# Chunked attention followed by a gated MLP: q in 1 KB runs, V products directly behind exp, turns of x ahead of all loads in the SyncE queue

## The chip, the cores and the metric

The kernel runs on one core of one Trainium2 chip. The metric is the device time of one execution in microseconds (us). A profile shows one execution; its span is about 1.7 us shorter than the device time of the same run.

## The reference

64 independent attention sequences (8 batches, 8 heads, 576 tokens, head size 64) attend within chunks of 64 tokens. The heads are put side by side into x (4608 tokens, 512 wide), and a gated MLP follows:

```python
scores = scale * np.matmul(q_c, k_c.transpose(0, 1, 2, 4, 3))   # per chunk of 64
attn = softmax(scores); out = np.matmul(attn, v_c)
x = out.transpose(0, 2, 1, 3).reshape(B * S, H * D)             # 4608 x 512
h = x @ w_in                                                    # 512 -> 2048
g = h * (1.0 / (1.0 + np.exp(-beta * h)))
return g @ w_out                                                # 2048 -> 512
```

Inputs and output are float32 in HBM; the kernel computes in bf16.

## The kernel before

x is cut into nine blocks, 0 to 8, of 512 tokens (block 8 collects the last 64 tokens of every batch). For each block TensorE does the *projections* (`mm1`, 64 matmuls of 512 columns) and the *output products* (`mm2`, 64 more). The attention of block b is woven into the output products of block b-1. It has these steps:

- 64 small *score* matmuls, then four exp on ScalarE;
- two halves of *V products*, 32 small matmuls each;
- normalization on VectorE, which makes x in four parts of 128 tokens;
- four DMA transposes, the *turns of x*, issued by SyncE. The projections of block b read the turned x (`xT`).

A list of (time, function) pairs is sorted, and each engine's queue is filled in that order. One time unit is one group of four output products or projections. SyncE issues every load of q, k, v and every turn from one in-order queue, so a load that stands before a turn there holds it up.

```python
def attention(blk, T):                     # T = 32 * blk - 16
    for u in range(2): at(T + 0.6, scores, blk, u)
    for i in range(4): at(T + 1 + 0.1 * i, exp, blk, i)
    for j in range(2):
        for m in (2 * j, 2 * j + 1):
            for u in range(2):
                at(T + 4.6 + 4 * j, attend, blk, m, u, A, 2 * (m % 2) + u)   # V products
            at(T + 4.7 + 4 * j, normalize, blk, m, (0, 1), A, 2 * (m % 2))
            at(T + 4.8 + 4 * j, turn_x, blk, m)

def prepare(blk, T):                       # loads, casts, turns of q and k
    for m in range(4):
        # ... (blocks 2 and 3 have lists of their own)
        late = 17.5 if blk in (4, 5) else 0
        when = (T - 48 + m, T - 44 + m, T - 40 + m + late), ...   # loads of q, k, v
        ...

def load(blk, name, m):                    # 128 tokens x 8 heads: runs of 64 floats, 256 B
    # ...
    drams[name][b, :, t:t + n, :].rearrange("h t d -> t h d")
```

The softmax here doesn't subtract the row's maximum and nothing guards it: scores larger than these inputs give would overflow.

Of the kernel before, what the change touches and what calls it, by code (L numbers as in the profile page):

```python
# [158 lines left out]
def bass_chunk_attention__then__act_swish_beta_kernel(nc, q, k, v, w_in, w_out, beta, out):  # L159
# [7 lines left out]
    with ExitStack() as es:  # L167
# [6 lines left out]
        warm = sb("warm", [128, 1], F32)  # L174
        beta_raw = sb("beta_raw", [128, 8, 2], F32)
        beta_half = sb("beta_half", [128, 8, 2], F32)
# [9 lines left out]
        x_sb = sb("x_sb", [128, 4, 512], BF16)  # L186
        xT = sb("xT", [128, 2, NC, 512], BF16)
        NTT = 4
        tt = sb("tt", [128, NTT, 512], BF16)
        g2 = sb("g2", [128, NT, 512], BF16)  # L190
        NOS = 3
        ostage = sb("ostage", [128, NOS, 512], F32)

# [19 lines left out]
        def make_identity():  # L213
            P.op("pool", lambda e: e.memset(warm0[:, :], 0.0), writes=[K("warm0")])
            P.op("pool", lambda e: e.memset(identity[:, :], 1.0), writes=[K("identity")])
            P.op("pool", lambda e: e.affine_select(
                out=identity[:, :], in_=identity[:, :], compare_op=ALU.is_equal, fill=0.0,
                base=0, pattern=[[-1, 128]], channel_multiplier=1),
                reads=[K("identity")], writes=[K("identity")])
            P.op("pool", lambda e: e.memset(vaug[:, :, :, 64:65], 1.0), writes=[K("ones")])  # L220

        def load_beta():
            def f(e):
                with nc.allow_non_contiguous_dma(reason="beta is tiny"):
                    return e.dma_start(beta_raw[:, :, :],
                                       beta.rearrange("(e p i) -> p e i", p=128, i=2))
            P.dma("sp", f, writes=[K("beta_raw")])

        def halve_beta():
            P.op("pool", lambda e: e.tensor_single_scalar(  # L230
                beta_half[:, :, :], beta_raw[:, :, :], 0.5, ALU.mult),
                reads=[K("beta_raw")], writes=[K("beta_half")])

# [43 lines left out]

        def load(blk, name, m):
            for r, n, b, t in pieces(blk, m):
                def f(e, r=r, n=n, b=b, t=t):  # L280
                    return e.dma_start(
                        stages[name][r:r + n, blk % 2, 512 * m:512 * m + 512].rearrange("p (h d) -> p h d", d=64),
                        drams[name][b, :, t:t + n, :].rearrange("h t d -> t h d"))
                P.dma("sp", f, writes=[K(name + "stage", blk % 2, m, r, v=blk)])

# [3 lines left out]
        def cast_qk(blk, name, m, eng):  # L289
            dst = cast[name][:, :].rearrange("p (h m x) -> p h m x", h=4, m=4)[:, :, m, :]  # L290
            src = stages[name][:, blk % 2, 512 * m:512 * m + 512].rearrange("p (h x) -> p h x", h=4)
            copy(eng, dst, src, stage_keys(blk, name, m),
                 [K(name + "cast", m, v=blk)] +
                 keys(name + "cast", (1, 2, 3) if blk == 2 and m == 0 else (), v=0))

# [46 lines left out]
        def scores(blk, u):  # L342
            for hp in (2 * u, 2 * u + 1):
                for m in range(4):
                    for h2, c2 in ((0, 0), (1, 1), (0, 1), (1, 0)):
                        bank, col = 2 * u + h2, ((hp % 2) * 4 + m) * 64

                        def f(e, hp=hp, h2=h2, c2=c2, bank=bank, col=col, m=m):
                            r = slice(64 * h2, 64 * h2 + 64)
                            t = slice(128 * m + 64 * c2, 128 * m + 64 * c2 + 64)  # L350
                            return e.matmul(A[64 * c2:64 * c2 + 64, bank, col:col + 64],  # L351
                                            turned["k"][r, hp, t], turned["q"][r, hp, t])
                        P.op("pe", f, reads=[K("qT", hp, v=blk), K("kT", hp, v=blk)],
                             writes=[K("A", bank, v=("s", blk))])

        def exp(blk, bank):
            P.op("act", lambda e: e.activation(E[:, bank, :], A[:, bank, :], AF.Exp, scale=0.125),  # L357
                 reads=[K("A", bank, v=("s", blk))], writes=[K("E", bank, v=blk)])
# [26 lines left out]
        def turn_x(blk, m):  # L385
            P.dma("sp", lambda e: e.dma_start_transpose(  # L386
                xT[:, blk % 2, :, 128 * m:128 * m + 128], x_sb[:, m, :]),
                reads=[K("x", m, u, v=blk) for u in range(2)],
                writes=[K("xT", blk % 2, m, v=blk)])

        def turn_x_pe(blk, m, ps, bank, eng):
            key = pkey(ps, bank)
            mid = ps[:, bank, 0:256].bitcast(BF16).rearrange("p (h t) -> p h t", h=4)
            for hp in range(4):
                P.op("pe", lambda e, hp=hp: e.transpose(  # L395
                    mid[:, hp, :], x_sb[:, m, 128 * hp:128 * hp + 128], identity[:, :]),
                    reads=[K("x", m, hp // 2, v=blk), K("identity")], writes=[K(*key, v=("x", blk, m))])
            copy(eng, xT[:, blk % 2, :, 128 * m:128 * m + 128], mid,
                 [K(*key, v=("x", blk, m))], [K("xT", blk % 2, m, v=blk)])

        def mm1(blk, t, lo=0, hi=512):
            bank, T = t % 4, NT * blk + t
            e0, i = t // 2, t % 2
            for c in range(NC):
                P.op("pe", lambda e, c=c: e.matmul(  # L405
                    F[:, bank, lo:hi], w_in_bf[:, c, 256 * e0 + i:256 * e0 + 256:2],
                    xT[:, blk % 2, c, lo:hi], start=(c == 0), stop=(c == NC - 1)),
                    reads=[K("w_in", e0, c)] +
                    [K("xT", blk % 2, m, v=blk) for m in range(lo // 128, hi // 128)],
                    writes=[K("F", bank, v=("h", T))])  # L410
# [30 lines left out]
        def attention(blk, T):  # L441
# [4 lines left out]
            for j in range(2):  # L446
                for m in (2 * j, 2 * j + 1):
                    for u in range(2):
                        at(T + 4.6 + 4 * j, attend, blk, m, u, A, 2 * (m % 2) + u)
                    at(T + 4.7 + 4 * j, normalize, blk, m, (0, 1), A, 2 * (m % 2))  # L450
                    at(T + 4.8 + 4 * j, turn_x, blk, m)

        def prepare(blk, T):
            for m in range(4):
                if blk == 2:
                    when = (26 + m, 30 + m, (34, 34.5, 35.5, 36)[m]), (30 + 0.8 * m, 34 + 0.4 * m, 40 + m), (33.5, 35.7)
                elif blk == 3:
                    when = (36.1 + 0.1 * m, (37.5, 37.6, 53, 53)[m], 58.1 + 0.1 * m), (44 + m, 48 + m + 6 * (m // 2), 70 + m), (58, 60)
                else:
                    late = 17.5 if blk in (4, 5) else 0  # L460
                    when = (T - 48 + m, T - 44 + m, T - 40 + m + late), \
                        (T - 41 + m, T - 37 + m, T - 17 + m + late / 5), (T - 20, T - 18)
                for i, name in enumerate("qkv"):
                    at(when[0][i], load, blk, name, m)
                    if name == "v":
                        at(when[1][i], cast_v, blk, m, "pool")
                    else:
                        at(when[1][i], cast_qk, blk, name, m, "pool")
                        if m == 3:
                            at(when[2][i], turn_qk, blk, name)  # L470

# [32 lines left out]
        at(-75, cast_w_in, 0, 1, ("pool", "pool"))  # L504
        at(-75, halve_beta)
        at(-75, cast_w_in, 1, 1, ("pool",))
# [97 lines left out]
```

## Time and profile before

| | before |
|---|---|
| device time, first three runs | 302.73 us median (302.0 to 303.44) |
| span of the profiled run | 300.8 us |
| first projection of block 0 / block 1 | 19.63 / 54.35 us |
| projections' start to projections' start, clean block | 29.90 us |
| the same into blocks 2, 5, 7 | 32.27, 31.23, 31.42 us |

The windows view of the kernel before follows, one line for each stretch from one block's first projection to the next one's (blocks 1-2, 2-3, 3-4, 4-5, 5-6, 6-7). The columns are the stretch, its length, then busy time (and instructions) of PE, PEld, DVE, ACT and POOL, then the granted TensorE clock, the DMA share and GB/s.

```profile
54.35:86.62 32.27, 30.34 (x272) 15.45 (x273) 14.57 (x25) 16.31 (x26) 9.97 (x17) 1.00 1.12 220
86.62:116.69 30.07, 30.05 (x256) 14.04 (x257) 14.41 (x24) 14.85 (x23) 7.25 (x12) 1.00 0.95 188
116.69:146.59 29.90, 29.90 (x257) 14.08 (x257) 14.41 (x24) 15.44 (x24) 7.36 (x12) 1.00 0.98 194
146.59:177.82 31.23, 30.06 (x257) 14.04 (x256) 14.41 (x24) 16.04 (x25) 9.81 (x16) 1.00 1.10 218
177.82:207.72 29.90, 29.89 (x256) 14.12 (x257) 14.41 (x24) 14.85 (x23) 7.30 (x12) 1.00 1.05 198
207.72:239.14 31.42, 30.06 (x258) 14.05 (x257) 14.41 (x24) 16.04 (x25) 7.36 (x12) 1.00 1.23 188
```

TensorE fills a clean block (29.90 of 29.90 us), so it is the limit there. VectorE and ScalarE are busy half the time. DMA is full (share about 1 and above). The surplus sits in three stretches, and the list of waits gives its cause (columns: us in total, times, longest):

```profile
PE F L405 <- DMA xT<-x_sb: 4.3, 3, 1.7
```

Three times TensorE was ready for the next block's projections and x had not been turned. The timeline of the kernel before around one of the three, at block 5, shows why. Its columns are start and length in us, the engine (SPq is SyncE's queue, DVE is VectorE), the line, the operation, out<-in (A and F lie in PSUM), shapes and count; in brackets stands how long the engine had been idle, and for what. DMA_DIRECT2D is a load, DMA_TRANSPOSE a turn.

```profile
163.90 5.03 SPq L281 DMA_DIRECT2D vstage<-in_v_dram  x4
165.61 0.70 PE L367 MATMUL A<-vaug,E 64*64 64x65 bf16 x32
166.34 0.69 DVE L379 TENSOR_TENSOR x_sb<-A,rden 128x512 bf16<-128x512 f32 x1
168.97 7.17 SPq L386 DMA_TRANSPOSE xT<-x_sb  x4
169.80 0.70 PE L367 MATMUL A<-vaug,E 64*64 64x65 bf16 x32
171.37 0.69 DVE L379 TENSOR_TENSOR x_sb<-A,rden 128x512 bf16<-128x512 f32 x1
177.82 2.53 PE L405 MATMUL F<-xT,w_in_bf 128*128 128x512 bf16 x11 [1.18 <-DMA xT<-x_sb]
```

Read it as a race. The first part of x is ready at 167.03 (166.34 + 0.69), but SyncE is still issuing v loads and comes to the turns at 168.97, 1.9 us late. The last part of x is ready at 172.06; TensorE wants all of it at 176.64 (177.82 - 1.18). Between these lie 4.6 us, in which the last turns must be issued and must land. They do not make it.

### The profile page before, as it was taken

How to read it: one execution, taken by the hardware profiler on the slowest of the kernel's cores; microseconds unless marked ns; L12 is line 12 of the kernel's file. 1: busy time of each engine (PE TensorE's matmuls, PEld its weight loads, DVE VectorE, ACT ScalarE, POOL GpSimd, SP SyncE). 2: the span in 40 equal slices, each digit the busy share in tenths (PEclk: the TensorE clock that was granted, in tenths of full speed). 3: DMA queues.
4: the chain of work that ended last, by engine and by line, in shares of the span. 5: the costliest groups of instructions: out<-in, count | busy, mean ns of one | idle time of the engine just before them, and what ended most of it. 6: DMA issues, size and time to landing. Idle time of an engine off the chain costs nothing.

```text
span 300.8 us, 5817 instructions
## 1 busy us (share of the span) xinstructions
PE 283.0 (94%) x2432; PEld 138.7 (46%) x2432; DVE 140.4 (47%) x238; ACT 148.6 (49%) x230; POOL 74.6 (25%) x118
## 2 busy tenths in 40 slices
PE   2789999999979999999999989999999899999994
PEld 1555454645434444444444534454444344444441
DVE  1547835483318442844274408541754076218600
ACT  3538624785138714871477037713871277228511
POOL 1347646332211521142114411440142100000000
PEclk9999999999999999999999999999999999999999
DMA  7999999999999948996999999998999950230033
GB/s 230 258 352 403 360 314 228 254 220 203 242 204 224 216 123 203 213 214 143 203 232 207 238 168 225 217 184 166 200 170 185 200 95 2 70 110 31 2 70 70
DMA packets 154489, 57.53 MB, mean 191 GB/s; under 512 B 142176, under 2 KB 147296, under 8 KB 154464
## 3 DMA queue, kind: packets, MB, share of 16 engines
q1 hardware_dynamic: 149216, 47.73, 79.0%
q10 hardware_dynamic: 5248, 9.44, 10.6%
q8 instruction: 19, 0.31, 0.5%
q14 instruction: 6, 0.05, 0.1%
HBM read 36.71 MB, written 9.44 MB: 153 GB/s over the span
## 4 chain that ended last, share of the span: by engine, by line
PE 85%; DMA 6%; DVE 4%; ACT 2%; SPq 1%; issue 1%
PE F L405 41%; PE F L424 36%; DMA xT<-x_sb 5%; PE A L367 3%; PE A L351 2%; DVE x_sb L379 2%; DMA kstage<-in_k_dram 2%; SPq L386 1%; ACT E L357 1%; DVE rden L377 1%; PE A L329 1%; PE F L329 1%; DVE g L417 0%; ACT tt L414 0%; PE F L395 0%
## 5 line engine op out<-in xcount | busy, mean ns | idle before, releaser
L417 DVE SCALAR_TENSOR_TENSOR g<-tt,F 128x512 bf16<-128x512 bf16 x144 | 98.5, 687 | 77.8 <-ACT tt L414 77.7
L405 PE MATMUL F<-xT,w_in_bf 128*128 128x512 bf16 (+1 forms) x608 | 127.2, 370 | 4.7 <-DMA xT<-x_sb 4.3
L424 PE MATMUL F<-w_out_bf,g 128*128 128x512 bf16 x576 | 130.6, 379 | 0.0
L414 ACT ACTIVATE tt<-F,beta_half 128x512 bf16<-128x512 f32 x144 | 98.3, 687 | 32.7 <-PE F L405 32.4
L405 PEld LDWEIGHTS F<-xT,w_in_bf 128*128 128x128 bf16 x608 | 59.5, 99 | 71.2 <-ACT ostage L429 3.5
L424 PEld LDWEIGHTS F<-w_out_bf,g 128*128 128x128 bf16 x576 | 54.2, 98 | 62.4
L429 ACT ACTIVATE ostage<-F 128x512 f32<-128x512 f32 x36 | 21.5, 597 | 92.2 <-PE F L424 92.0
L260 POOL CAST vaug<-vstage 128x512 bf16<-128x512 f32 x36 | 22.8, 634 | 67.8 <-DMA vstage<-in_v_dram 57.6
L260 POOL CAST qcast<-qstage 128x512 bf16<-128x512 f32 x28 | 17.2, 613 | 52.7 <-DMA qstage<-in_q_dram 51.7
L377 DVE RECIPROCAL rden<-A 128x8 f32<-128x8 f32 (+1 forms) x36 | 7.2, 200 | 49.2 <-PE A L367 49.2
L260 POOL CAST kcast<-kstage 128x512 bf16<-128x512 f32 (+1 forms) x30 | 19.3, 642 | 30.6 <-DMA kstage<-in_k_dram 30.6
L379 DVE TENSOR_TENSOR x_sb<-A,rden 128x512 bf16<-128x512 f32 (+1 forms) x36 | 23.8, 662 | 1.2
L357 ACT ACTIVATE E<-A 128x512 bf16<-128x512 f32 x36 | 18.8, 601 | 8.4 <-PE A L351 8.4
L367 PEld LDWEIGHTS A<-vaug,E 64*64 64x64 bf16 x544 | 10.6, 109 | 8.3 <-issue 3.8
L367 PE MATMUL A<-vaug,E 64*64 64x65 bf16 x544 | 13.1, 195 | 0.8 <-ACT E L357 0.5
L260 POOL CAST w_in_bf<-wstage 128x1024 bf16<-128x1024 f32 (+1 forms) x9 | 8.3, 945 | 5.1 <-DMA wstage<-in_moe_w_in_dram 5.1
L351 PEld LDWEIGHTS A<-qT,kT 64*64 64x64 bf16 x576 | 6.4, 111 | 5.7 <-issue 3.4
L351 PE MATMUL A<-qT,kT 64*64 64x64 bf16 x576 | 7.9, 200 | 1.2 <-DVE kT L260 0.7
L329 PE MATMUL F<-identity,qcast 128*128 128x128 bf16 x16 | 2.0, 308 | 5.5 <-DVE qcast L260 5.5
L260 POOL CAST w_out_bf<-wstage 128x1024 bf16<-128x1024 f32 x6 | 6.1, 1041 | 2.9 <-DMA wstage<-in_moe_w_out_dram 2.0
L258 ACT ACTIVATE qT<-F 128x1024 bf16<-128x1024 bf16 x2 | 2.0, 1023 | 5.8 <-PE F L329 5.8
L260 DVE CAST qcast<-qstage 128x1024 bf16<-128x1024 f32 x4 | 2.7, 694 | 4.7 <-DMA qstage<-in_q_dram 4.7
(38 smaller groups left out, 38.7 us busy)
## 6 DMA issues: line engine op xcount, KB each, us to landing
vstage<-in_v_dram SPq DMA_DIRECT2D x32, 256.0 KB, 5.1
out_dram<-ostage ACTq DMA_DIRECT2D x32, 256.0 KB, 3.6
qstage<-in_q_dram SPq DMA_DIRECT2D x24, 256.0 KB, 5.0
kstage<-in_k_dram SPq DMA_DIRECT2D x24, 256.0 KB, 5.8
wstage<-in_moe_w_out_dram SPq DMA_DIRECT2D x4, 1024.0 KB, 11.9
wstage<-in_moe_w_in_dram SPq DMA_DIRECT2D x3, 1024.0 KB, 9.6
qstage<-in_q_dram SPq DMA_DIRECT2D x4, 512.0 KB, 9.7
kstage<-in_k_dram SPq DMA_DIRECT2D x4, 512.0 KB, 8.4
```

What stands on the lines that cost most here:

```text
L260: P.op(eng, lambda e: e.tensor_copy(dst, src), reads=r, writes=wr)
L329: P.op("pe", lambda e, h=h, i=i, c=c, mid=mid: e.transpose(mid[:, 512 * h + 128 * i:512 * h + 128 * i + 128], cast[name][:, c:c + 128], id ...
L351: return e.matmul(A[64 * c2:64 * c2 + 64, bank, col:col + 64], turned["k"][r, hp, t], turned["q"][r, hp, t])
L357: P.op("act", lambda e: e.activation(E[:, bank, :], A[:, bank, :], AF.Exp, scale=0.125), reads=[K("A", bank, v=("s", blk))], writes=[K("E" ...
L367: return e.matmul(ps[r, bank, 128 * (h % 4):128 * (h % 4) + 65], E[r, 2 * u + h % 2, col:col + 64], vaug[r, m, h, 0:65])
L377: P.op("dve", lambda e: e.reciprocal(rd, o[:, :, :, 64]), reads=r, writes=[K("rden", m, u, v=blk) for u in us])
L379: P.op("dve", lambda e: e.tensor_tensor(x_sb[:, m, 256 * us[0]:256 * (us[0] + n)].rearrange("p (b h d) -> p b h d", h=4, b=n), o[:, :, :, ...
L405: P.op("pe", lambda e, c=c: e.matmul(F[:, bank, lo:hi], w_in_bf[:, c, 256 * e0 + i:256 * e0 + 256:2], xT[:, blk % 2, c, lo:hi], start=(c = ...
L414: P.op("act", lambda e: e.activation(tt[:, T % NTT, :], F[:, bank, :], AF.Tanh, scale=beta_half[:, e0, i:i + 1]), reads=[K("F", bank, v=(" ...
L417: P.op("dve", lambda e: e.scalar_tensor_tensor(g2[:, t, :], tt[:, T % NTT, :], 1.0, F[:, bank, :], ALU.add, ALU.mult), reads=[K("F", bank, ...
L424: P.op("pe", lambda e, t=t: e.matmul(F[:, s, :], g2[:, t, 128 * s:128 * s + 128], w_out_bf[:, t, :], start=(t == 0), stop=(t == NT - 1)), ...
L429: P.op("act", lambda e: e.activation(ostage[:, N % NOS, :], F[:, s, :], AF.Copy, scale=0.5), reads=[K("F", s, v=("o", N))], writes=[K("o", ...
```

## The change

The intent is to have the turns land in time by three means, and to relieve the DMA. The diff, cut to its core:

```diff
 def attention(blk, T):
-    at(T + 4.6 + 4 * j, attend, ...)      at(T + 4.7 + 4 * j, normalize, ...)    at(T + 4.8 + 4 * j, turn_x, ...)
+    at(T + 4.1 + 2.5 * j, attend, ...)    at(T + 4.2 + 2.5 * j, normalize, ...)  at(T + 4.3 + 2.5 * j, turn_x, ...)
 def prepare(blk, T):                       # other lists of times
+    late = {3: 12}.get(blk, 0)
+    lq, lk = [T - 48 + late + u for u in range(2)], [T - 46 + late + m for m in range(4)]
+    lv = [T - 42 + late * 1.6 + m for m in range(4)]
+    ...
+    if spread(blk):                        # 2 <= blk < 8
+        at(lq[u], load_qk4, blk, "q", u)   # four tokens x 64 floats in one run: 1 KB
+        at(cq[u], cast_qk4, blk, "q", u, "pool")
 def scores(blk, u):                        # moving operand: four runs of 16 tokens
+    qq = turned["q"][r, 2*u:2*u+2, :].rearrange("d a (b h p) -> d h (a b) p", b=2, h=2)[:, hp % 2, :, 16*c:16*c+16]
 def exp(blk, bank):                        # puts the tokens in order while it reads PSUM
+    dst = dst.rearrange("k (g p i) -> k g p i", p=16, i=4)
+    src = src.rearrange("k (g i p) -> k g p i", p=16, i=4)
-xT = sb("xT", [128, 2, NC, 512], BF16)     # and five output stages instead of three
+xT = sb("xT", [128, NC, 512], BF16)
-beta_raw: one load of 128x8x2 (runs of 8 B)
+beta_raw: four loads of 8x64 (runs of 256 B) and two 32x32-block transposes on VectorE
```

On TensorE only 8 instead of 16 output products stand between the two halves of the V products; in SyncE's queue the four turns of x stand together, and from block 4 on a period carries four turns, the turns of the next q and k, then the loads of q, k, v of the block after.

More of the change, by code (lines that the diff above doesn't have):

```diff
@@ L174, in bass_chunk_attention__then__act_swish_beta_kernel @@
         warm = sb("warm", [128, 1], F32)
-        beta_raw = sb("beta_raw", [128, 8, 2], F32)
+        beta_raw = sb("beta_raw", [128, 64], F32)
+        beta_turned = sb("beta_turned", [128, 2, 32], F32)
         beta_half = sb("beta_half", [128, 8, 2], F32)
@@ L190, in bass_chunk_attention__then__act_swish_beta_kernel @@
         g2 = sb("g2", [128, NT, 512], BF16)
-        NOS = 3
+        NOS = 5
         ostage = sb("ostage", [128, NOS, 512], F32)
@@ L219, in make_identity @@
                 reads=[K("identity")], writes=[K("identity")])
+            P.op("pool", lambda e: e.memset(beta_raw[:, :], 0.0), writes=[K("beta_pad")])
             P.op("pool", lambda e: e.memset(vaug[:, :, :, 64:65], 1.0), writes=[K("ones")])
         def load_beta():
-            def f(e):
-                with nc.allow_non_contiguous_dma(reason="beta is tiny"):
-                    return e.dma_start(beta_raw[:, :, :],
-                                       beta.rearrange("(e p i) -> p e i", p=128, i=2))
-            P.dma("sp", f, writes=[K("beta_raw")])
+            for g in range(4):
+                P.dma("sp", lambda e, g=g: e.dma_start(
+                    beta_raw[32 * g:32 * g + 8, :],
+                    beta.rearrange("(e x) -> e x", e=8)[:, 64 * g:64 * g + 64]),
+                    reads=[K("beta_pad")], writes=[K("beta_raw", g)])
         def halve_beta():
+            for i in range(2):
+                P.op("dve", lambda e, i=i: e.transpose(beta_turned[:, i, :], beta_raw[:, i::2]),
+                     reads=[K("beta_raw", g) for g in range(4)], writes=[K("beta_turned", i)])
             P.op("pool", lambda e: e.tensor_single_scalar(
-                beta_half[:, :, :], beta_raw[:, :, :], 0.5, ALU.mult),
-                reads=[K("beta_raw")], writes=[K("beta_half")])
+                beta_half[:, :, :], beta_turned[:, :, 0:8].rearrange("p i e -> p e i"), 0.5, ALU.mult),
+                reads=[K("beta_turned", i) for i in range(2)], writes=[K("beta_half")])
         def load_w_in(e0, n):
@@ L275, in cast_w_out, with load @@
                      [K("w_out", t + x) for x in range(n)])
-        def load(blk, name, m):
+        def load(blk, name, m, eng="sp"):
             for r, n, b, t in pieces(blk, m):
@@ L283, in f @@
                         drams[name][b, :, t:t + n, :].rearrange("h t d -> t h d"))
-                P.dma("sp", f, writes=[K(name + "stage", blk % 2, m, r, v=blk)])
+                P.dma(eng, f, writes=[K(name + "stage", blk % 2, m, r, v=blk)])
         def stage_keys(blk, name, m):
@@ L293, in cast_qk, with spread @@
                  [K(name + "cast", m, v=blk)] +
-                 keys(name + "cast", (1, 2, 3) if blk == 2 and m == 0 else (), v=0))
+                 keys(name + "cast", (1, 2, 3) if m == 0 and blk in (2, B) else (), v=0))
+        def spread(blk):
+            return 2 <= blk < B
         def turn_qk(blk, name):
@@ L349, in f @@
                             r = slice(64 * h2, 64 * h2 + 64)
-                            t = slice(128 * m + 64 * c2, 128 * m + 64 * c2 + 64)
+                            c = 2 * m + c2
+                            t = slice(64 * c, 64 * c + 64)
+                            qq = turned["q"][r, hp, t]
+                            if spread(blk):
+                                qq = turned["q"][r, 2 * u:2 * u + 2, :].rearrange(
+                                    "d a (b h p) -> d h (a b) p", b=2, h=2)[
+                                    :, hp % 2, :, 16 * c:16 * c + 16]
                             return e.matmul(A[64 * c2:64 * c2 + 64, bank, col:col + 64],
-                                            turned["k"][r, hp, t], turned["q"][r, hp, t])
+                                            turned["k"][r, hp, t], qq)
                         P.op("pe", f, reads=[K("qT", hp, v=blk), K("kT", hp, v=blk)],
@@ L356, in exp @@
         def exp(blk, bank):
-            P.op("act", lambda e: e.activation(E[:, bank, :], A[:, bank, :], AF.Exp, scale=0.125),
+            dst, src = E[:, bank, :], A[:, bank, :]
+            if spread(blk):
+                dst = dst.rearrange("k (g p i) -> k g p i", p=16, i=4)
+                src = src.rearrange("k (g i p) -> k g p i", p=16, i=4)
+            P.op("act", lambda e: e.activation(dst, src, AF.Exp, scale=0.125),
                  reads=[K("A", bank, v=("s", blk))], writes=[K("E", bank, v=blk)])
@@ L386, in turn_x @@
             P.dma("sp", lambda e: e.dma_start_transpose(
-                xT[:, blk % 2, :, 128 * m:128 * m + 128], x_sb[:, m, :]),
+                xT[:, :, 128 * m:128 * m + 128], x_sb[:, m, :]),
                 reads=[K("x", m, u, v=blk) for u in range(2)],
-                writes=[K("xT", blk % 2, m, v=blk)])
+                writes=[K("xT", m, v=blk)])
         def turn_x_pe(blk, m, ps, bank, eng):
@@ L397, in turn_x_pe @@
                     reads=[K("x", m, hp // 2, v=blk), K("identity")], writes=[K(*key, v=("x", blk, m))])
-            copy(eng, xT[:, blk % 2, :, 128 * m:128 * m + 128], mid,
-                 [K(*key, v=("x", blk, m))], [K("xT", blk % 2, m, v=blk)])
+            copy(eng, xT[:, :, 128 * m:128 * m + 128], mid,
+                 [K(*key, v=("x", blk, m))], [K("xT", m, v=blk)])
         def mm1(blk, t, lo=0, hi=512):
@@ L406, in mm1 @@
                     F[:, bank, lo:hi], w_in_bf[:, c, 256 * e0 + i:256 * e0 + 256:2],
-                    xT[:, blk % 2, c, lo:hi], start=(c == 0), stop=(c == NC - 1)),
+                    xT[:, c, lo:hi], start=(c == 0), stop=(c == NC - 1)),
                     reads=[K("w_in", e0, c)] +
-                    [K("xT", blk % 2, m, v=blk) for m in range(lo // 128, hi // 128)],
+                    [K("xT", m, v=blk) for m in range(lo // 128, hi // 128)],
                     writes=[K("F", bank, v=("h", T))])
@@ L448, in attention @@
                     for u in range(2):
-                        at(T + 4.6 + 4 * j, attend, blk, m, u, A, 2 * (m % 2) + u)
-                    at(T + 4.7 + 4 * j, normalize, blk, m, (0, 1), A, 2 * (m % 2))
-                    at(T + 4.8 + 4 * j, turn_x, blk, m)
+                        at(T + 4.1 + 2.5 * j, attend, blk, m, u, A, 2 * (m % 2) + u)
+                    at(T + 4.2 + 2.5 * j, normalize, blk, m, (0, 1), A, 2 * (m % 2))
+                    at(T + 4.3 + 2.5 * j, turn_x, blk, m)
         def prepare(blk, T):
-            for m in range(4):
-                if blk == 2:
-                    when = (26 + m, 30 + m, (34, 34.5, 35.5, 36)[m]), (30 + 0.8 * m, 34 + 0.4 * m, 40 + m), (33.5, 35.7)
-                elif blk == 3:
-                    when = (36.1 + 0.1 * m, (37.5, 37.6, 53, 53)[m], 58.1 + 0.1 * m), (44 + m, 48 + m + 6 * (m // 2), 70 + m), (58, 60)
-                else:
-                    late = 17.5 if blk in (4, 5) else 0
-                    when = (T - 48 + m, T - 44 + m, T - 40 + m + late), \
-                        (T - 41 + m, T - 37 + m, T - 17 + m + late / 5), (T - 20, T - 18)
-                for i, name in enumerate("qkv"):
-                    at(when[0][i], load, blk, name, m)
-                    if name == "v":
-                        at(when[1][i], cast_v, blk, m, "pool")
-                    else:
-                        at(when[1][i], cast_qk, blk, name, m, "pool")
-                        if m == 3:
-                            at(when[2][i], turn_qk, blk, name)
@@ new lines, in prepare @@
+            if blk == 2:
+                lq, lk, lv = (26, 27), (30, 31, 32, 33), (34, 34.5, 35.5, 36)
+                cq, ck, cv = (28, 30), (34, 34.4, 34.8, 35.2), (40, 41, 42, 43)
+                turns = (33.5, 35.7)
+            else:
+                late = {3: 12}.get(blk, 0)
+                lq, lk = [T - 48 + late + u for u in range(2)], [T - 46 + late + m for m in range(4)]
+                lv = [T - 42 + late * 1.6 + m for m in range(4)]
+                cq, ck = [T - 41 + late + u for u in range(2)], [T - 39 + late + m for m in range(4)]
+                cv = [T - 13 + m for m in range(4)]
+                turns = T - 20, T - 18
@@ new lines, in prepare @@
+            for u in range(2):
+                if spread(blk):
+                    at(lq[u], load_qk4, blk, "q", u)
+                    at(cq[u], cast_qk4, blk, "q", u, "pool")
+                else:
+                    for m in (2 * u, 2 * u + 1):
+                        at(lq[u], load, blk, "q", m)
+                        at(cq[u], cast_qk, blk, "q", m, "pool")
+            for m in range(4):
+                at(lk[m], load, blk, "k", m)
+                at(ck[m], cast_qk, blk, "k", m, "pool")
+                at(lv[m], load, blk, "v", m)
+                at(cv[m], cast_v, blk, m, "pool")
@@ L473, in bass_chunk_attention__then__act_swish_beta_kernel @@
+            at(turns[0], turn_qk, blk, "q")
+            at(turns[1], turn_qk, blk, "k")
         first = (("q", 0), ("k", 0), ("q", 1), ("k", 1))
@@ L504, in bass_chunk_attention__then__act_swish_beta_kernel @@
         at(-75, cast_w_in, 0, 1, ("pool", "pool"))
-        at(-75, halve_beta)
+        at(-69.2, halve_beta)
         at(-75, cast_w_in, 1, 1, ("pool",))
```

## The prediction

> **What bounds the kernel now.** TensorE. The windows view gives PE 30.05 us busy of 30.07 us from projection start to projection start of a steady block (86.6 to 116.7 us), clock 1.00. The same period takes 31.07 us into block 5 (146.8 to 177.8), 31.26 us into block 7 (207.9 to 239.1) and 32.27 us into block 2. The list of waits names the surplus: PE's first projection waited for the transposed x, 4.3 us in 3 waits (timeline: 1.74, 1.18, 1.36 us at 86.6, 177.8, 239.1). PE's other idle time is the start (about 9 of the first 19.6 us) and the end (about 4 us), which the change hardly touches.
>
> **Why those waits.** The chain there: x by VectorE, two x turns issued by SyncE (1.22, 1.26 us), then 3.05, 4.50 and (block 2) 6.70 us of DMA. DMA is full: share 0.95 to 1.23 in these windows. In block 2 two k loads stand between the turns; into blocks 5 and 7 SyncE reaches the first turn about 2 and 1.3 us after x was ready, because eight v loads stood before it.
>
> **What changes.**
> 1. q of blocks 2 to 7 in 1 KB runs. In the trace a 256 B packet takes 23.0 ns on average, a 1 KB one 51.4. 1 MB of q costs 4096 x 23.0 / 16 = 5.9 us of DMA before, 1024 x 51.4 / 16 = 3.3 after: 2.6 us less per block, none directly on PE's path. The Trainium skill, "DMA: Bandwidth & Descriptors", Specifications, puts line rate at 512 B and more; the packets agree (11 against 20 GB/s per engine).
> 2. Its price: scores stream q in runs of 16 tokens, exp reads PSUM with a stride. I expect both unchanged (64 score matmuls in 0.69 us, exp 601 ns); no strided PSUM read by exp is in the trace. Slack: exps end at 72.2 us, V products start at 73.85.
> 3. Second half of the V products 8 instead of 16 matmuls after the first: 1.7 us earlier. Normalization frees its banks about 0.5 us before.
> 4. Four x turns together. Counted from the V products' start: x ready after 1.4 to 4.6 us, last turn issued by 6.5, landed by 9.5 to 11; PE needs it at 10.8. It just fits.
> 5. beta as four small loads plus two VectorE transposes: 1024 packets x 9.2 ns / 16 = 0.6 us of DMA saved, perhaps 1 us more SyncE issue. The start's chain does not contain it: near 0.
> 6. One xT buffer: the turn follows the last projection of the block before anyway. Free.
>
> **On the critical path:** only the 4.3 us of x waits. I expect 4.1 gone: 302.7 - 4.1 = 298.6 us. Range 297.2 to 300.4. Chances: faster by over 2% 0.05, within 2% 0.92, slower 0.03.
>
> **Signs.** Right: PE waits for transposed x below 0.5 us in all; every period from block 2 on 30.0 to 30.1 us; first projection still at about 19.6 us; DMA share per period down by about 0.08; score group 0.69 us, exp about 600 ns. Wrong: scores or exp slower; x turns landing over 4.5 us after the last issue; a PE wait for exp or normalization between the V products; first projections waiting for w_in.
>
> **What would break it.** A strided moving operand that halves the score rate costs 0.7 us x 6 = 4 us and eats the gain. A DMA backlog ahead of the x turns of block 2 or 3 (v of two blocks there) leaves a wait of 1 to 2 us.

## The result, and the profile after

The change runs in 298.8 us (median of 4 runs, 298.38 to 299.22), the kernel before in 302.37 us (4 runs). The ratio is 0.988, with a 95% interval of 0.9844 to 0.9917. Ratios here are the mean time of one kernel's runs over that of the other's of the same rounds, so they are not quite the ratio of the medians. The whole interval lies below 1, so the change is faster, but by less than 2%.

The windows view of the changed kernel, same stretches and columns as above:

```profile
55.27:85.57 30.30, 29.56 (x267) 15.60 (x273) 14.56 (x25) 15.46 (x25) 8.21 (x12) 1.00 1.03 210
85.57:116.19 30.62, 29.75 (x253) 14.03 (x256) 14.40 (x24) 15.97 (x25) 9.44 (x14) 1.00 1.14 224
116.19:146.09 29.90, 29.58 (x253) 14.12 (x258) 14.40 (x24) 14.92 (x24) 6.88 (x10) 1.00 0.97 196
146.09:175.99 29.90, 29.58 (x254) 14.09 (x257) 14.41 (x24) 15.45 (x24) 6.88 (x10) 1.00 0.89 193
175.99:205.88 29.89, 29.57 (x253) 14.08 (x256) 14.40 (x24) 15.45 (x24) 6.88 (x10) 1.00 0.97 195
205.88:235.78 29.90, 29.58 (x254) 14.11 (x256) 14.40 (x24) 15.45 (x24) 7.36 (x12) 1.00 1.16 192
```

The stretches into blocks 5 and 7 are clean now, and the one into block 2 lost 1.97 us. (PE's busy time reads 0.3 us less than the stretch because some matmul records are missing: 253 instead of 256.) The one into block 3 became 0.55 us longer. The list of waits of the changed kernel names what is left:

```profile
PE F L424 <- DMA xT<-x_sb: 0.6, 1, 0.6
```

The timeline of the changed kernel at block 5, to be read as the one above:

```profile
165.11 0.70 PE L386 MATMUL A<-vaug,E 64*64 64x65 bf16 x32
165.84 0.69 DVE L398 TENSOR_TENSOR x_sb<-A,rden 128x512 bf16<-128x512 f32 x1
166.56 6.27 SPq L405 DMA_TRANSPOSE xT<-x_sb  x4
167.57 0.70 PE L386 MATMUL A<-vaug,E 64*64 64x65 bf16 x32
169.14 0.69 DVE L398 TENSOR_TENSOR x_sb<-A,rden 128x512 bf16<-128x512 f32 x1
175.99 4.26 PE L424 MATMUL F<-xT,w_in_bf 128*128 128x512 bf16 x19
```

SyncE waits for x (it issues at 166.56, x was ready at 166.53). The last part of x is ready at 169.83, 6.2 us before TensorE wants it. It was 4.6 before, 1.6 us less. The second V products moved by 1.7 us; 0.15 us of it is not seen because TensorE lost that much more before than the list of waits shows (31.23 - 29.90 - 1.18).

**The account.** From block 1's first projection to the end, the kernel before takes 300.8 - 54.35 = 246.45 us and the changed one 297.5 - 55.27 = 242.23 us: 4.22 us less. The 0.92 us that separate this from the 3.3 us between the two spans were lost before block 1, in the start (54.35 against 55.27); that is put down to chance, the moment at which TensorE's full clock came (see the experiments on the start).

**The price of the 1 KB runs** was to be in scores and exp. The groups of both kernels (columns: count, busy us, mean ns of one, then idle time before) show none. Before:

```profile
L357 ACT ACTIVATE E<-A 128x512 bf16<-128x512 f32 x36 | 18.8, 601 | 8.4 <-PE A L351 8.4
L351 PE MATMUL A<-qT,kT 64*64 64x64 bf16 x576 | 7.9, 200 | 1.2 <-DVE kT L260 0.7
```

After:

```profile
L376 ACT ACTIVATE E<-A 128x512 bf16<-128x512 f32 x36 | 18.8, 601 | 8.4 <-PE A L366 8.4
L366 PE MATMUL A<-qT,kT 64*64 64x64 bf16 x576 | 7.9, 200 | 1.1 <-DVE kT L266 0.7
```

24 of the 36 exps (blocks 2 to 7) have the new form, and the four of each block take 592 to 619 ns in both kernels. Neither ScalarE's strided read of PSUM nor q in runs of 32 B, as TensorE now streams it, cost anything here.

### The profile page after: what moved, and what is told of

It reads as the page before. It is cut to its first block, busy times and chain, and to the rows that moved or that the text cites. A ratio compares the mean times of both kernels' runs of the same rounds, so it can differ in the third digit from the quotient of the medians.

```text
span 297.5 us, 5766 instructions
## 1 busy us (share of the span) xinstructions
PE 280.0 (94%) x2395; PEld 139.3 (47%) x2432; DVE 140.6 (47%) x240; ACT 148.5 (50%) x230; POOL 72.2 (24%) x107
## 4 chain that ended last, share of the span: by engine, by line
PE 81%; SPq 8%; DMA 6%; issue 2%; DVE 1%; ACT 0%; POOL 0%
PE F L443 39%; PE F L424 37%; DMA kstage<-in_k_dram 5%; PE A L386 3%; SPq L287 3%; PE A L366 2%; SPq L247 1%; DMA xT<-x_sb 1%; SPq L405 1%; SPq L319 1%; SPq L271 1%; DVE x_sb L398 1%; PE A L338 1%; SPq L227 0%; POOL kcast L266 0%
## 5 line engine op out<-in xcount | busy, mean ns | idle before, releaser
L443 PE MATMUL F<-w_out_bf,g 128*128 128x512 bf16 x548 | 127.4, 379 | 2.4 <-issue 1.3
L448 ACT ACTIVATE ostage<-F 128x512 f32<-128x512 f32 x36 | 21.5, 597 | 92.0 <-PE F L443 92.0
L266 POOL CAST qcast<-qstage 128x1024 bf16<-128x1024 f32 (+1 forms) x16 | 14.9, 934 | 68.8 <-DMA qstage<-in_q_dram 68.8
L266 POOL CAST kcast<-kstage 128x512 bf16<-128x512 f32 (+1 forms) x30 | 19.3, 644 | 21.5 <-DMA kstage<-in_k_dram 21.4
```

The lines of the kernel that those rows point to most:

```text
L266: P.op(eng, lambda e: e.tensor_copy(dst, src), reads=r, writes=wr)
L443: P.op("pe", lambda e, t=t: e.matmul(F[:, s, :], g2[:, t, 128 * s:128 * s + 128], w_out_bf[:, t, :], start=(t == 0), stop=(t == NT - 1)), ...
L448: P.op("act", lambda e: e.activation(ostage[:, N % NOS, :], F[:, s, :], AF.Copy, scale=0.5), reads=[K("F", s, v=("o", N))], writes=[K("o", ...
```

## The experiments

Three parts of the change can be switched one by one: q in 1 KB runs (**q**), the earlier V products (**V**), the new order of loads and turns in the queue, with the casts that follow the loads (**order**). Each was left out of the change and each was run alone. The rest of the change (beta, one xT, five output stages) was not switched by itself: it is in the runs that leave one part out, and not in those with one part alone. The table puts these runs and the later v_later together. "Into block n" is the time from the previous block's first projection to block n's, from the timeline; into blocks 4, 6 and 8 it is 29.86 to 29.90 us in every profile. "From block 1" is the span less the start of block 1's projections, so it does not contain the start. Each profile is one execution, while the median is of 4 runs (of the kernel before, 4 to 11 in four sets).

| run | parts | into 2 | into 3 | into 5 | into 7 | from block 1 | median | ratio to before |
|---|---|---|---|---|---|---|---|---|
| before | none | 32.27 | 30.07 | 31.23 | 31.42 | 246.45 | 302.2 to 303.1 | |
| q_only | q | 32.54 | 30.08 | 31.10 | 31.42 | 246.67 | 302.12 | 0.9975 |
| order_only | order | 31.76 | 30.70 | 29.90 | 30.39 | 244.22 | 301.11 | 0.9963 |
| attn_only | V | 31.58 | 29.89 | 30.20 | 29.90 | 243.12 | 300.27 | 0.9926 |
| no_q | V, order | 30.76 | 32.05 | 29.90 | 29.90 | 244.14 | 300.81 | 0.9935 |
| old_order | q, V | 31.60 | 29.90 | 30.34 | 29.90 | 243.24 | 300.37 | 0.9922 |
| old_attn | q, order | 31.16 | 30.44 | 29.90 | 29.90 | 242.88 | 299.48 | 0.9884 |
| the change | all | 30.30 | 30.62 | 29.90 | 29.90 | 242.23 | 298.80 | 0.988 |
| v_later | all, v later | 30.30 | 29.90 | 29.90 | 29.90 | 241.50 | 298.15 | 0.984 |

### One part left out, and q alone

The edits, each against the changed kernel, except the last, which puts the 1 KB runs into the kernel before:

```diff
 no_q:       -    return 2 <= blk < B
             +    return False
 old_attn:   -    at(T + 4.1 + 2.5 * j, attend, ...)   (and 4.2, 4.3 likewise)
             +    at(T + 4.6 + 4 * j, attend, ...)     (and 4.7, 4.8 likewise)
 old_order:  the times of the kernel before in prepare(), with load_qk4 / cast_qk4 for q
 q_only:     the kernel before, with spread(), load_qk4 / cast_qk4, the new scores() and exp()
```

Expected of no_q:

> The change without its 1 KB runs: q of blocks 2 to 7 in 256 B runs again, everything else as changed. Theory A (the x turns come early enough because the second V products are 1.7 us earlier and the turns stand together ahead of the loads; q only relieves a DMA that is not waited for): PE waits for transposed x at most 1 us in all, about 299.3 us. Rival B (the gain is the 15.7 us of DMA time that the 1 KB runs free): waits of 2 to 4 us come back, 301 to 303 us.

Measured: 300.81 us (ratio 0.9935, 0.989 to 0.998), x waits 2.3 us in all, 2.0 of them at block 3. Theory A is refuted: the 1 KB runs are needed. Rival B's waits of 2 to 4 us did come back and its time was missed by 0.2 us, but the waits do not show its reason, DMA time that is missing everywhere: nearly all is at one block. The timeline of no_q before block 3 shows it:

```profile
93.98 3.51 SPq L287 DMA_DIRECT2D qstage<-in_q_dram  x4
97.53 5.34 SPq L287 DMA_DIRECT2D kstage<-in_k_dram  x4
102.92 5.23 SPq L287 DMA_DIRECT2D vstage<-in_v_dram  x4
105.16 0.69 DVE L398 TENSOR_TENSOR x_sb<-A,rden 128x512 bf16<-128x512 f32 x1
108.19 7.74 SPq L405 DMA_TRANSPOSE xT<-x_sb  x4
117.47 1.89 PE L424 MATMUL F<-xT,w_in_bf 128*128 128x512 bf16 x8 [2.00 <-DMA xT<-x_sb]
```

x is ready at 105.85, and SyncE comes at 108.19: between the turns of blocks 2 and 3 the new order issues v of block 3 and q, k, v of block 4, 4 MB, where every later period has 3 MB. With the 1 KB runs the two q loads take 1.13 us of issue instead of 3.51, and SyncE comes at 106.38.

Expected of old_attn:

> The change with the old places of the V products (second half 16 projections' matmuls after the first, its x turns 1.7 us later). Theory A: the last turn is issued about 8.2 us after the V products' start instead of 6.5 and the projections want it at 10.8 to 11, so where landing takes over 2.5 us there is a wait: blocks 2 and 3 1 to 2 us each, the others 0 to 0.5; 300 to 301.5 us. Rival B: as the change, 298.8 us.

Measured: 299.48 us (0.9884, 0.9831 to 0.9937). The stretch into block 2 grew from 30.30 to 31.16 us, and no wait came back at blocks 5 and 7. By its median the run fell below A's 300 to 301.5 us, and its waits (0.70 us at block 2, 0.39 at block 3) were smaller than A expected. By the time alone rival B is not excluded: the ratio is 0.9884 here and 0.988 for the change. V's own share, from one profile of each, is 0.65 us here (242.88 - 242.23).

Expected of old_order:

> The change with the old order of loads in the SyncE queue (k loads between the turns of block 2, v of two blocks in one period ahead of turns), q still in 1 KB runs, V products still early. Theory A, in the form that the place in the queue matters: SyncE reaches the first turn up to 2 us late into blocks 5 and 7 and waits of 0.5 to 1.5 us remain, 300 us or more. Rival B: the freed DMA time lets SyncE arrive in time, waits below 0.7 us, about 299 us.

Measured: 300.37 us (0.9922, 0.9874 to 0.997). The waits listed are 1.13 us at block 2, where two k loads stand between the turns again, and 0.28 us at block 5; block 7 is clean. Theory A's time was met, though the large share is block 2, not blocks 5 and 7 as it said.

Expected of q_only:

> The kernel before with nothing but q of blocks 2 to 7 in 1 KB runs and exp putting the tokens in order. Rival B: the three waits for transposed x (1.74, 1.18, 1.36 us) shrink to below 1 us in all, 299 to 299.5 us. Theory A: block 2 keeps at least 1 us and the total stays above 2 us, 300.5 us or more. Both: score group 0.69 us and exp 601 ns, as before.

Measured: 302.12 us (0.9975, 0.9913 to 1.0037), x waits 3.5 us in all (1.07, 1.05, 1.37): theory A was right here, rival B was wrong. The DMA time was freed, and it was not what was missing. The timeline of q_only at block 5:

```profile
166.89 0.69 DVE L392 TENSOR_TENSOR x_sb<-A,rden 128x512 bf16<-128x512 f32 x1
167.75 7.37 SPq L399 DMA_TRANSPOSE xT<-x_sb  x4
171.92 0.69 DVE L392 TENSOR_TENSOR x_sb<-A,rden 128x512 bf16<-128x512 f32 x1
174.41 0.37 ACTq L445 DMA_DIRECT2D out_dram<-ostage  x1
178.25 2.10 PE L418 MATMUL F<-xT,w_in_bf 128*128 128x512 bf16 x9 [1.05 <-DMA xT<-x_sb]
```

SyncE now comes 0.2 us after x instead of 1.9. But the wait hardly moved. Three things are late. The last part of x is still ready only at 172.61, 4.6 us before TensorE wants it. The first turn, directly behind the v loads, held the queue for 3.4 us, so that the last one was issued from 173.85 to 175.12. And that one landed only at 178.12, 3.0 us later; while it was in flight, an output (`out_dram`, 256 KB, issued by ScalarE at 174.41) was moved. Which of them made the wait q_only alone cannot tell, but order_only (below) has x as late and no wait at block 5:

```profile
168.00 6.69 SPq L389 DMA_TRANSPOSE xT<-x_sb  x4
172.31 0.69 DVE L382 TENSOR_TENSOR x_sb<-A,rden 128x512 bf16<-128x512 f32 x1
174.81 0.36 ACTq L435 DMA_DIRECT2D out_dram<-ostage  x1
177.43 2.75 PE L408 MATMUL F<-xT,w_in_bf 128*128 128x512 bf16 x12
```

Here the last turn was issued by 174.69, just ahead of the output, and landed 1.2 us later, at 175.92. So late x alone makes no wait there. The output is an influence that none of the texts before the runs considered. By the packet records of all 14 profiles, a block's last turn landed 1.2 to 1.5 us after the end of its issue where no packet of an output went in between (44 turns), and 2.1 to 3.2 us after it where 100 or more of an output's 128 packets did (16 turns). For the wait that the change has left at block 3 it was 2.1 us with 86 packets. No run moved the outputs, so this stays a correlation.

### V alone, order alone

```diff
 attn_only:  the kernel before
             -    at(T + 4.6 + 4 * j, attend, ...)     (and 4.7, 4.8 likewise)
             +    at(T + 4.1 + 2.5 * j, attend, ...)   (and 4.2, 4.3 likewise)
 order_only: the kernel before, with the changed prepare(), spread() always False
```

Expected of attn_only:

> The kernel before with nothing but the earlier second V products (and their x turns). After the first four runs the theory is C: a turn of x is late when any one of three things is late, x itself, SyncE, or the landing behind loads in flight, so one part alone moves little. C expects: block 2 about 1.1 us of wait left (as with the old order of loads), blocks 5 and 7 0.5 to 1.2 us each since SyncE still arrives 1 to 2 us late; 2 to 3.5 us in all, about 301 us. Rival D (the early V products alone do it, q and order are decoration): waits below 1 us in all, 299 us.

Measured: 300.27 us (0.9926, 0.9873 to 0.9979). Block 2 kept a wait of 1.1 us, as C expected, block 5 kept 0.3 us of stretch (30.20 against 29.90), block 7 nothing. The view puts the wait at block 2 down to ScalarE's copy of the outputs (`ACT ostage`):

```profile
87.16 13.97 PE L405 MATMUL F<-xT,w_in_bf 128*128 128x512 bf16 x64 [1.11 <-ACT ostage L429]
```

It is a wait for x all the same: the last turn landed at 87.06, and where the list names x, TensorE starts just as closely, 0.1 to 0.25 us, after the last landing. The same holds for the waits so labelled in order_only and v_later_no_q, and for the 0.70 us of old_attn. Theory C ("one part alone moves little") was refuted here: V alone gives 3.3 of the 4.2 us from block 1 on. Rival D was nearer, but its 299 us and "below 1 us in all" were missed because of block 2.

Expected of order_only:

> The kernel before with nothing but the new order of loads and turns in the SyncE queue (q in 256 B runs, V products at the old places). It closes the table of three parts, alone and left out. From the first projection of block 1 to the end, the profiles gave 246.4 us before, 246.7 with q alone, 243.1 with the early V products alone, 242.2 with all, and 244.1, 242.9, 243.2 with q, V products, order left out. Theory G (the new order alone clears blocks 5 and 7 but pays at block 3, where 4 MB stand before the turns): a wait of 2 us or more at block 3, 0 to 1.5 us at block 2, none at 5 and 7; 245 to 246 us there. Rival H (the order alone is worth as much as the V products alone): 243 to 244 us there and no wait over 1 us.

Measured: 301.11 us (0.9963, 0.9926 to 1.0), 244.22 us from block 1. Three waits stand in its timeline: 1.29 us at block 2 and 0.65 at block 3 (both labelled `ACT ostage`, with the last turn landing 0.20 and 0.13 us before TensorE starts) and 0.33 at block 7. Neither theory was met: of G's numbers only block 2's held, and H's no wait over 1 us fails there. The order alone gives 2.2 us, half of the gain. The 4 MB before block 3 made a wait of 0.65 us here and of 2.0 in no_q; why it differs so was not tested.

**What follows.** The gains do not add: -0.2 (q), 2.2 (order) and 3.3 (V) alone sum to 5.3, together they make 4.2. V and order are largely two ways to win the same race, while q is worth nothing alone, about nothing beside V (243.12 against 243.24 us), and 1.9 us (244.14 - 242.23) once the order has put 4 MB before block 3's turns. Without q, V and order together (no_q, 244.14 us) are 1.0 us slower than V alone (243.12): there the new order costs more than it gives. (These are single profiles, and no_q has the untested rest of the change and attn_only has not.)

### Removing the last wait, and where the 1 KB runs pay

The explanation of no_q says what to do about the 0.56 us that the change has left at block 3: move v behind the turns, so that each period carries 3 MB.

```diff
 v_later:
-    lv = [T - 42 + late * 1.6 + m for m in range(4)]
+    lv = [T - 42 + late * 1.6 + m if blk == 3 else T - 17 + 0.1 * m for m in range(4)]
 v_later_no_q:  v_later with spread() always False
 v_later_q23:   v_later with  return 2 <= blk < 4
 v_later_q47:   v_later with  return 4 <= blk < B
```

(For the last two, the block at which the form of q changes waits for all pieces of the cast, as block 2 did.)

> The change with the v loads of blocks 4 to 8 moved behind the x turns of the block before, so that no period between x turns carries more than 3 MB of loads. Theory C: the wait of 0.56 us that the change has left at block 3 goes, every period from block 2 on is 29.9 us; measured from the first projection of block 1 the rest takes 241.7 us instead of 242.2; about 298.3 us. Rival E (that wait is not made by the 4 MB between the turns of blocks 2 and 3): it stays at 0.4 us or more.

Measured: 298.15 us (0.984, 0.9809 to 0.9871); 241.50 us from block 1. No wait for x is listed any more, and every stretch after the one into block 2 is 29.9 us. The timeline of v_later at block 3 has no load between the k loads and the turns:

```profile
93.85 5.58 SPq L287 DMA_DIRECT2D kstage<-in_k_dram  x4
105.27 6.21 SPq L405 DMA_TRANSPOSE xT<-x_sb  x4
114.70 4.48 PE L424 MATMUL F<-xT,w_in_bf 128*128 128x512 bf16 x20
```

The four turns took 6.21 us to issue; in the change, with v loads just ahead of them, 7.59. Theory C held and rival E was refuted. This version is faster than the kernel before. Against the change the profiles give 0.73 us from block 1 on; the 0.65 us of median are from different rounds and the intervals of the ratios overlap, so the times alone do not show it.

> As v_later, but with q in 256 B runs again. Theory C, in the form that the 1 KB runs pay only for the 4 MB period before block 3: its wait of 2.0 us (seen without the 1 KB runs) goes, at most 0.3 us of wait stays at block 2, and the time is within 0.5 us of v_later. Rival F (the freed DMA time is needed as such): 1.5 us or more slower than v_later.

Measured: 300.25 us (0.9907, 0.9876 to 0.9939). As expected the stretch into block 3 is clean (29.89). But the run is 2.1 us slower than v_later, as rival F said, so theory C's "within 0.5 us" was missed, and so was its "at most 0.3 us" at block 2: there TensorE waited 0.66 us for the last turn (under the label `ACT ostage`), and the stretch took 31.13 us against 30.30. The spans of the two profiled executions differ by 1.8 us, 0.9 from block 1 on and 0.9 before it, where the full clock came 2.0 us later (see the start). So only about 0.9 us is seen to be the 1 KB runs' own.

> v_later with 1 KB runs for q of blocks 2 and 3 only. v_later and v_later_no_q differed by 2.1 us in their medians, though the profiles differ only before block 2 (0.83 us in the period from block 1 to block 2, the rest in the start). If the 1 KB runs pay only where the loads of the start still fill the DMA: within 0.5 us of v_later (298.2 us). If they pay in all blocks: about 299.5 us.

Measured: 298.46 us (6 runs, 0.9878, 0.9846 to 0.991); into block 2 30.30 us, 241.54 us from block 1. In the profile and by its median this is as v_later; by the ratio (0.984 there) it is 1.1 us behind, from different rounds and with overlapping intervals.

> v_later with 1 KB runs for q of blocks 4 to 7 only: the counterpart of v_later_q23. If the 1 KB runs pay only in the first blocks: as v_later_no_q, 299.3 to 300.3 us, with a wait of 0.3 to 1 us at block 2. If they pay in all blocks: about 299 us or less.

Measured: 299.18 us (6 runs, 0.9919, 0.9875 to 0.9963); into block 2 30.88 us with 0.41 us of listed wait, all else clean, 242.06 us from block 1. The direction is as expected, the median a little below the range, with one run at 302.22.

So, as far as single profiles show, the 1 KB runs pay at q of blocks 2 and 3, whose loads share the DMA with the end of the start and stand before the turns of block 2, and they change no later stretch in the profiles of v_later and its variants. By the times the case is not closed: the intervals of q23 and q47 overlap.

### The start

In the start of block 1's projections the profiles differ by 2.1 us (54.35 to 56.46 us). The windows of TensorE at the first projections, before:

```profile
20.00:22.00 2.00, 2.00 (x14) 1.48 (x12) 0.00 (x0) 0.47 (x1) 0.45 (x1) 1.00 1.04 390
22.00:24.00 2.00, 2.00 (x21) 1.73 (x18) 0.35 (x1) 1.07 (x2) 1.58 (x2) 1.00 1.05 389
```

and after:

```profile
20.00:22.00 2.00, 2.00 (x11) 1.44 (x10) 0.00 (x0) 0.60 (x1) 0.41 (x2) 1.00 1.05 390
22.00:24.00 2.00, 2.00 (x15) 1.55 (x14) 0.00 (x0) 0.15 (x1) 1.77 (x2) 1.00 1.05 387
```

The same matmuls come at 14 and 21 per 2 us before, and at 11 and 15 after, at the same busy time. The trace's clock records say why: full clock from 21.5 us on before, from 23.2 after, and from 21.7 to 25.4 us in the other profiles; block 1 starts at 54.4 to 54.7 us where it came before 22 us, and at 56.3 and 56.5 us in two of the three profiles where it came after 24 (55.6 in the third). Half the clock (0.5 in the records) makes each us of such matmuls cost half a us, so the 1.7 us between before and after explain about 0.85 of the 0.92 us between their starts of block 1 (an estimate from these numbers). The change alone does not set the moment: attn_only, which has the start of the kernel before, got its full clock at 24.7 us, and v_later, which has the changed one, at 21.7. The Trainium skill, "TensorE: Matmul & The Clock Gate", Part 1, says that the clock rises after a busy window of about 3.4 us that is free-running and does not start with the kernel. That fits: every stretch at full clock that the records give is a whole number of times 3.413 us (80, 81, 82 and 85 times, and once in v_later_warm). The 1.00 in the clock column before the first record only says that no record stands there.

Two runs tried to bring the full clock forward:

```diff
 v_later_warm: 38 matmuls of the identity on itself into bank A0, before the first transposes
 v_later_keep_warm: the same, and 59 more (12, 12, 3, 14, 12, 6) in the gaps up to the first V products
```

> v_later with 38 matmuls of the identity matrix on itself at the start, in a bank that the first scores overwrite, while TensorE would wait for the first loads anyway. The records give TensorE's full clock from 21.5 us (before) to 25.4 us on, and block 1's projections start at 54.35 to 56.5 us in step with it. If the clock comes with sustained work, it comes before 9 us here, block 1 starts at about 52.5 to 53.5 us, and the time is about 296 us; the runs also scatter less. If not, 298.3 us as v_later.

Measured: 298.98 us (4 runs, 297.84 to 300.15; 0.9868, 0.9826 to 0.991), block 1 at 54.91 us: the expected 296 us, the earlier block 1 and the smaller scatter were all missed. The clock did come at 4.77 us, and it was lost at 8.18, 3.41 us later, until 21.83. The windows view of v_later_warm shows the loss in the clock column (third from the right):

```profile
6.00:8.00 2.00, 0.72 (x10) 0.45 (x8) 1.31 (x3) 1.42 (x2) 0.00 (x0) 1.00 1.06 343
8.00:10.00 2.00, 1.64 (x40) 1.27 (x40) 0.94 (x3) 0.40 (x2) 0.00 (x0) 0.55 1.28 260
10.00:12.00 2.00, 1.16 (x9) 0.90 (x9) 1.12 (x2) 2.00 (x4) 0.61 (x1) 0.50 1.20 209
20.00:22.00 2.00, 2.00 (x12) 1.43 (x11) 0.00 (x0) 0.20 (x1) 0.36 (x1) 0.54 1.05 395
```

> v_later_warm got the full clock at 4.77 us and lost it again at 8.18 us, until 21.83. Here 59 more such matmuls fill TensorE's gaps between 6 and 13 us. If the clock stays with a TensorE that has no long gaps: full clock from about 5 to 8 us on without a break (or with one short one), block 1's projections at 52.5 to 53.5 us instead of 54.5 to 55.5, about 296.5 us. If the fillers hold up the transposes and scores instead, or the clock is lost all the same: 298 us or more.

Measured: 297.97 us (6 runs, 0.9857, 0.9826 to 0.9888), no better than v_later's ratio of 0.984. In the profiled execution the clock was full from 5.69 us on without a break, and the first projection came at 18.30 instead of 19.73 us. But block 1 started at 55.11 us, not at 52.5 to 53.5. The list of waits of this run has one that v_later does not have:

```profile
PE F L429 <- POOL w_in_bf L271: 1.6, 1, 1.6
```

The projections now waited for w_in, whose cast ended at 20.90 us after a load (19.76 in v_later), in a start whose DMA share is 1.0 and more. A faster TensorE reached the next limit, the loads. Whether the fillers also slowed these loads or whether that is chance was not tested. Nor is this profile typical: its execution has a mean clock of 0.998 and took 298.7 us, while the other five have 0.987 to 0.988 and took 297.27 to 298.05. That means about 6 us more at half clock in each (an estimate: 0.0105 x 296 us / 0.5), so the clock was probably lost again in those five, which no profile shows. The one execution that is known to have kept it was the slowest.

## Why the prediction was right

- **The time.** 298.6 us were predicted, 298.8 measured, within 297.2 to 300.4. That it is so close is partly luck: the prediction took 4.1 us from 302.73, the first three runs' median, while the four runs measured beside the change have 302.37, so the medians differ by 3.6 us.
- **What bounds it, and the 4.3 us of x waits on the critical path:** right. 3.7 of the 4.3 us of waits went; in stretches, block 1 to the end lost 4.22 us, since each wait had cost about 0.15 us more than the list shows (31.23 - 29.90 - 1.18). (The prediction's 31.07 and 31.26 us into blocks 5 and 7 are measured from 0.16 us after the first projection; from projection to projection they are 31.23 and 31.42. Its 3.05, 4.50 and 6.70 us of DMA count from the start of a turn's issue, so they contain 1.3 to 3.1 us of issue.)
- **V products 1.7 us earlier, turns together, "it just fits":** right. Counted from the V products' start at block 5, the last turn was issued from 6.45 to 7.71 us (predicted "by 6.5"), landed at 8.94 ("9.5 to 11") and was needed at 10.88 ("10.8"). V is the strongest part alone (3.3 us), but either V or the order clears block 5 by itself to within 0.3 us, so the prediction's sum of all parts is not a sum of needed parts. Normalization freed the banks not 0.5 but 0.2 us ahead of the second V products (167.37 and 167.57); TensorE did not wait.
- **q "none directly on PE's path":** right alone (q_only: nothing), but incomplete. Without the 1 KB runs the changed kernel waits 2.0 us at block 3. The prediction had costed the DMA time (2.6 us per MB; with the packets after, 23.3 and 52.1 ns, it is still 2.6) but not that the new order would spend it. The 4 MB were named under "what would break it", as 1 to 2 us, and 0.56 us were left.
- **Scores and exp unchanged:** right (200 and 601 ns, both times).
- **The signs.** "Waits below 0.5 us in all" was missed narrowly (0.6), "30.0 to 30.1 us from block 2 on" on both sides (29.9, and 30.62 into block 3). "DMA share down by 0.08" holds roughly for the stretches into blocks 2, 5, 6 and 7, 0.07 to 0.21 less, hardly for block 4 (0.97 against 0.98), and not for the one into block 3, which got a larger share (1.14 against 0.95) with its 4 MB. None of the signs against it came: scores and exp are unchanged, the last turn landed at most 3.4 us after SyncE began to issue it, and no first projection waited for w_in.
- **The start, "near 0":** right for the first projection (19.63 and 19.79). The 0.9 us lost up to block 1 is chance, the clock's timing, as far as the other profiles tell; no run fixed the clock to show it. The beta loads took 1.46 us of SyncE's issue instead of 0.74, without a wait to show for it. Beta, the single xT and the five output stages were not tested alone.

## What to carry to other kernels

A transfer that is late has three things in a row that can be late: its data, the queue that issues it, and its landing. Relieving one can show nothing (q alone) or most of the gain (V alone), so compare all three with the moment at which the result is wanted before choosing, and look at what other transfers are in flight at the landing. And a reordered in-order queue should be counted in bytes between deadlines: one period with 4 MB instead of 3 ate what the 1 KB runs had freed.

## What the Trainium skill lacked or had wrong

- "DMA: Bandwidth & Descriptors", Issuing engines are not separate DMA queues: it calls the time to initiate a DMA usually small relative to the DMA itself. Here, in the kernel before, a turn of x (128x512 bf16) held SyncE's queue for 1.26 us in the median (1.19 to 3.08), against 3.3 us in the median from the start of the issue to landing, and in the changed kernel four in a row, with what they wait for, took 5.7 to 7.6 us.
- The same page, Specifications: 512 B as the least size for line rate agrees in direction. The packets of the kernel before took 23.0 ns at 256 B, 51.4 at 1 KB, 104.5 at 2 KB and 164.9 at 4 KB, which is 11, 20, 20 and 25 GB/s per engine, so 1 KB is still short of the rate at 4 KB. (Each size belongs to other transfers, so this is no clean test of size.)
- "PSUM — Partial Sum Buffer", Specifications, warns that a non-contiguous access pattern slows matmuls, and has nothing on strided reads by ScalarE. ScalarE's read with a step of 64 B took 601 ns for 128x512, the same as contiguous.
- "TensorE: Matmul & The Clock Gate", Part 1, gives about ±500 ns of scatter for the rise of the clock. Here it came between 21.5 and 25.4 us in kernels whose starts are nearly the same, 1.9 to 5.0 us after the first projection, a spread of nearly one window. The 3.41 us for which v_later_warm held the clock agree with the page's window of 3413 ns.
